# An attention and two-layer kernel whose hand-kept order is computed anew with other prices for DMA and GpSimd

## The chip, the core and the metric

The kernel runs on one core of a Trainium2 chip. The metric is the device time in microseconds of one execution. All work is in 32-bit floats.

## The reference

Attention within chunks of 64 tokens feeds two layers of a feed-forward network without a router. Cut to what is computed:

```python
scores = (1 / sqrt(64)) * q_c @ k_c.T            # 4 x 8 heads, 9 chunks of 64 tokens
attn = softmax(scores); x = attn @ v_c           # 2304 tokens x 512
r = maximum(x @ w_in, 0); x = (s * (r * r) + b) @ w_out        # first layer, 512 -> 2048 -> 512
h = x @ w_in2; g = maximum(h, 0) + log1p(exp(-abs(h)))         # second layer
out = g @ w_out2
```

The weights arrive in 64-bit floats and are converted on the chip.

## The kernel before

**Stages.** The kernel goes through five stages: attention over 18 tiles of 128 tokens (`attention`, `held`), the first product of layer one (`quad0`), its second product (`second`, phase 0), the first product of layer two (`quad1`) and its second product (phase 1). Each product of two matrices is done in blocks with seven products in place of eight, so sums and differences of blocks are made on VectorE (DVE) and GpSimd (POOL), and each operand is split into a high and a low part (`split`: a cast on ScalarE, L1077, and a subtraction, L1086). Meanwhile weights are loaded and converted (`weights1`, `weights2`).

**A quad.** `quad0 i j` (and `quad1 i j`) takes 256 columns of weights, number i of 8, and 384 tokens, group j of 3. Its steps are numbered here in the order in which the function adds them, in brackets. The seven products on TensorE, each of six matmuls (L1487), are [0], [2], [4], [7], [11], [14], [17]; [1], [5] copy a sum to the next bank on ScalarE (L1509); [3] copies it to the buffer `s2` (ScalarE or VectorE, L887 or L889); [6] and [8] subtract on VectorE (L1064). The results leave the banks through ScalarE as [9], [12], [15], [18] (L1520) into buffers of kind `go` (five places; every other quad from number 6 on uses `g1`, in layer two `g2` and `g3`), and are squared in place as [10], [13], [16], [19] (L1532 or L1534). Four adds or subtractions follow, [23] to [26], three of which claim a further buffer. Seven stores of 192 KB to DRAM, [20], [21], [22] and [27] to [30] (L905), free the buffers: that of [9] is free after [24] and store [20]; of [12] after [25] and [21]; of [15] after [26] and [22]; of [18] after store [28]. The second product loads these results again (`second`, step [0], 768 KB).

**What sets the order.** Each function adds steps (`Op`) to a list, 3587 in all, of which 726 are TensorE's. The table `PLAN`, written out in the source, gives each step a rank by its turn and number, with V or G behind it where the step goes to VectorE or GpSimd instead of its default engine. `order` sorts each engine's steps by rank: this is the engine's order, and every engine keeps to it strictly. `order` also steps through a picture of the machine (prices of engines, a DMA queue) to choose which of a kind's places each step gets, and in which interleaving the engines' steps are emitted. All loads and stores are issued by SyncE (SP) on one queue. The loads of `s` and `b` (L1986, L1987, 0.5 KB each, one value to each of 128 partitions) are not ranked: they are emitted behind the last step of `x_ready[0, 2]`, which is `held 8`[11].

Of the kernel before, what the change touches and what calls it, by code (L numbers as in the profile page):

```python
# [610 lines left out]
class Work:  # L611
# [8 lines left out]
    BANKS = "A", "S", "at"  # L620
    HELD = {"DVE": 0.06, "POOL": 0.1}
    STORE, LOAD, FIRST = 1.6, 2.3, 3.0
    BYTES = 330e3

    COLD = 7.0

# [34 lines left out]
    def order(self, places):  # L661
# [7 lines left out]
        memory = port = 0.0  # L669
# [84 lines left out]
def block_attention_two_layers(  # L754
# [36 lines left out]
    work = Work()  # L791
# [462 lines left out]
    held = {}  # L1254
# [799 lines left out]
```

## Time and profile before

| | us |
|---|---|
| median of 3 runs | 813.82 |
| lowest and highest | 811.82, 817.78 |
| the profiled execution | 814.79 |
| its span, first to last instruction | 813.0 |
| TensorE busy | 775.7 (95%) |
| VectorE busy | 671.7 (83%) |
| ScalarE busy | 533.3 (66%) |
| GpSimd busy | 126.1 (16%) |

The profile is of one execution. PE is TensorE, DVE VectorE, ACT ScalarE, POOL GpSimd, SP SyncE, whose queue issues the DMAs. An engine is busy while an instruction of it is executed; the idle time before an instruction is put down to what ended it. An L and a number is a line of the kernel; L1064 and L905 are helpers that many steps share, so a step is told from its neighbours by its place in time and in the order of its engine.

### The profile page before, as it was taken

To read this page: it belongs to the slowest core of one execution; us is meant where nothing else is said; L and a number is where in the kernel's file an instruction comes from. 1 tells how busy PE (TensorE), PEld (TensorE's weight loads), DVE (VectorE), ACT (ScalarE), POOL (GpSimd) and SP (SyncE) were. 2 spreads that over 40 slices of the span, in tenths; PEclk is the share of its full clock that TensorE was granted. 3 is DMA by queue.
4 is the path that set the end of the run, shared out by engine and by line. 5 is a ranking of instruction groups with operands and counts; after the bars stand their busy time and mean duration, and the time that the engine had idled before them with its cause. 6 is when DMAs were issued, how large, how long until landed. Compare 5 with 4: busy or idle time off the path is not lost.

```text
span 813.0 us, 14302 instructions
## 1 busy us (share of the span) xinstructions
PE 775.7 (95%) x4995; PEld 750.5 (92%) x4995; DVE 671.7 (83%) x1181; ACT 533.3 (66%) x1068; POOL 126.1 (16%) x132
## 2 busy tenths in 40 slices
PE   6898899999988799999999899999999999999998
PEld 5687798899987799999999899999999999999997
DVE  6999898999896798987999979999865766567674
ACT  6998888889876777665677856565555455445451
POOL 4444001222212110000104221212200000000000
PEclk9999999999999999999999999999999999999999
DMA  7766388999999997988875068998788897558743
GB/s 243 246 211 211 133 289 252 312 311 326 312 317 298 324 331 307 338 291 286 295 237 193 11 229 297 311 322 266 271 286 291 303 383 257 204 230 267 282 162 136
DMA packets 97112, 214.86 MB, mean 264 GB/s; under 512 B 10384, under 2 KB 70800, under 8 KB 96144
## 3 DMA queue, kind: packets, MB, share of 16 engines
q1 hardware_dynamic: 97040, 213.95, 77.2%
q8 instruction: 39, 0.64, 0.3%
q14 instruction: 33, 0.27, 0.1%
HBM read 128.45 MB, written 85.46 MB: 263 GB/s over the span
## 4 chain that ended last, share of the span: by engine, by line
PE 63%; DVE 8%; DMA 6%; ACT 5%; issue 2%; POOL 0%; SPq 0%; DVEq 0%; ACTq 0%; POOLq 0%
PE S L1755 15%; PE at L1755 15%; PE at L1487 13%; PE A L1755 10%; PE S L1487 6%; DMA summed<-mem 5%; PE A L1487 4%; DVE mem L1064 2%; DVE operands L1086 2%; ACT mem L1520 1%; ACT operands L1077 1%; DMA last<-summed 1%; DVE last L1086 1%; ACT mem L956 1%; ACT mem L1532 1%
## 5 line engine op out<-in xcount | busy, mean ns | idle before, releaser
L1755 PE MATMUL S<-operands 128*128 128x384 f32 (+1 forms) x768 | 176.4, 337 | 4.8 <-ACT mem L1520 4.7
L1755 PE MATMUL at<-operands 128*128 128x384 f32 (+1 forms) x768 | 175.3, 335 | 0.0
L1086 DVE TENSOR_TENSOR operands<-mem,operands 128x768 fp32r<-128x768 f32 (+3 forms) x150 | 132.8, 908 | 41.3 <-ACT operands L1077 40.8
L1077 ACT CAST operands<-mem 128x768 fp32r<-128x768 f32 (+3 forms) x150 | 115.3, 792 | 72.4 <-PE at L1755 39.0
L1064 POOL TENSOR_TENSOR mem<-mem 128x256 f32<-128x256 f32 (+1 forms) x95 | 92.2, 978 | 432.3 <-DVE mem L1044 229.9
L1077 ACT CAST operands<-last 128x768 fp32r<-128x768 f32 (+2 forms) x136 | 103.8, 781 | 81.1 <-PE at L1755 39.2
L1064 DVE TENSOR_TENSOR mem<-mem 128x384 f32<-128x384 f32 (+1 forms) x261 | 131.6, 521 | 25.1 <-DMA summed<-mem 9.5
L1755 PEld LDWEIGHTS S<-operands 128*128 128x128 f32 x768 | 137.3, 189 | 6.4 <-ACT mem L1520 5.3
L1086 DVE TENSOR_TENSOR operands<-last,operands 128x768 fp32r<-128x768 f32 (+2 forms) x132 | 118.5, 914 | 25.0 <-ACT operands L1077 24.2
L1755 PEld LDWEIGHTS at<-operands 128*128 128x128 f32 x768 | 137.7, 189 | 0.0
L1487 PE MATMUL at<-operands 128*128 128x384 f32 x624 | 120.7, 337 | 4.5 <-ACT S L1509 3.5
L1487 PEld LDWEIGHTS at<-operands 128*128 128x128 f32 x624 | 108.5, 188 | 8.3 <-ACT S L1509 4.9
L1755 PE MATMUL A<-operands 128*128 128x384 f32 (+1 forms) x480 | 89.3, 335 | 0.0
L1487 PE MATMUL S<-operands 128*128 128x384 f32 x420 | 85.0, 338 | 2.3 <-DVE S L1064 2.3
L1755 PEld LDWEIGHTS A<-operands 128*128 128x128 f32 x480 | 83.9, 188 | 0.1
L1487 PEld LDWEIGHTS S<-operands 128*128 128x128 f32 x420 | 74.3, 189 | 3.0 <-DVE S L1064 2.7
L1520 ACT ACTIVATE mem<-S 128x384 f32<-128x384 f32 x104 | 50.7, 490 | 36.7 <-DMA summed<-mem 13.8
L1487 PE MATMUL at<-last,operands 128*128 128x384 f32 x336 | 68.6, 341 | 2.9 <-DVE mem L889 1.3
L1487 PE MATMUL A<-operands 128*128 128x384 f32 x300 | 62.5, 346 | 7.2 <-DVE A L1064 4.5
L1487 PEld LDWEIGHTS at<-last,operands 128*128 128x128 f32 x336 | 59.1, 188 | 5.3 <-ACT S L1509 1.8
L1487 PEld LDWEIGHTS A<-operands 128*128 128x128 f32 x300 | 52.7, 191 | 11.3 <-DVE A L1064 5.7
L956 ACT ACTIVATE mem<-mem 128x512 f32<-128x512 int32 x88 | 55.5, 631 | 1.6 <-DVE mem L947 0.8
(101 smaller groups left out, 891.2 us busy)
## 6 DMA issues: line engine op xcount, KB each, us to landing
summed<-mem SPq DMA_DIRECT2D x336, 192.0 KB, 3.6
last<-summed SPq DMA_DIRECT2D x54, 768.0 KB, 5.9
mem<-in_w_dram SPq DMA_DIRECT2D x64, 512.0 KB, 4.9
mem<-summed SPq DMA_DIRECT2D x30, 768.0 KB, 6.2
last<-in_qk_dram SPq DMA_DIRECT2D x36, 256.0 KB, 4.0
forms<-mem SPq DMA_DIRECT2D x16, 512.0 KB, 5.0
mem<-forms SPq DMA_DIRECT2D x7, 1024.0 KB, 7.5
mem<-forms SPq DMA_DIRECT2D x12, 512.0 KB, 6.5
```

What stands on the lines that cost most here:

```text
L956: return lambda e: nc.scalar.activation(out=out(), in_=in_(), func=AF.Prelu, scale=scale, bias=bias, alpha=alpha)
L1064: lambda e: on(e).tensor_tensor(out=out(), in0=x(), in1=y(), op=op or ALU.subtract),
L1077: lambda e: nc.scalar.copy(out=hi().bitcast(F32R), in_=x()),
L1086: lambda e: on(e).tensor_tensor(out=lo().bitcast(F32R), in0=x(), in1=hi(), op=ALU.subtract),
L1487: nc.tensor.matmul(acc(dst)().rearrange("p (u c) -> p u c", u=GROUP), l[a], r[c], start=start and kk == 0 and x == 0, stop=kk == 1 and x == 2,
L1520: lambda e: nc.scalar.activation(out=at(go), in_=acc(place)(), func=AF.Softplus if ph else AF.Relu),
L1532: nc.scalar.activation(out=at(go), in_=at(go), func=AF.Square)
L1755: nc.tensor.matmul(at(accs[d])[:, :width], l[a], r[c], start=i == 0 and y == 0, stop=i == NF - 1 and y == 2,)
```

## The change

The picture of the machine has other prices. A store is taken to land 1.9 us after its data have moved (before 1.6), a load 1.9 (2.3), a load of attention 2.8 (3.0); the queue moves 365 KB/us (330), and a load behind a store costs 0.6 us more. A step on GpSimd is priced higher. `PLAN` is replaced for the most part: ranks and engine marks; the last part of the table stays. Operations and shapes are the same. Of the table, the rows that the prediction speaks of stand here.

```diff
-    STORE, LOAD, FIRST = 1.6, 2.3, 3.0
-    BYTES = 330e3
+    STORE, LOAD, FIRST = 1.9, 1.9, 2.8
+    BYTES, TURN = 365e3, 0.6
...
+        op.store = False
...
                 memory = max(memory, t + cost) + op.late / self.BYTES
+                if stored and not op.store:
+                    memory += self.TURN
+                stored = op.store
...
-    return Port(0.135 + n * (0.0017 if spread else 0.00214))
+    return Port(0.2 + n * (0.0018 if spread else 0.0025))
...
-            op.lag = work.STORE
+            op.lag, op.store = work.STORE, True
...
-    "held 8": "410 433 401 420 394 426 443 438G 432 446 447 457",
+    "held 8": "403 430 405 409 407 415 443 435G 429 439 453 458",
-    "quad0 1 0": "388 397 400 408 411 419 423 430 439 436 445 417 428 434 424 442 450 449 461 464 458 437 454 467 473 475 481 471 477 479 484",
+    "quad0 1 0": "388 396 401 408 412 419 424 428 437 434 438 406 421 445 422 436 441 440 457 460 448 451 444 463 468 473 478 485 471 477 482",
-    "quad0 0 1": "406 440 444 452 456 466 470 474 482 491 496V 468 483 487 480 493 501V 486 495 504 500 503 507 509 515 521 523 513 519 524 528",
+    "quad0 0 1": "433 442 447 456 459 467 470 474 483 490 495V 465 481 484 479 498 504 489 496 501 499 503 508 505 510 519 522 511 516 529 526",
-    "weights2 0 0": "465 494V 497 508 499 505 511 490 516 520 532 525 531 537 543 546 517G 549 553 564 560",
+    "weights2 0 0": "464 491V 492 506 493 497 513 488 518 521 533 523 530 536 542G 549 540 554 561 564 558",
-    "quad0 3 2": "800 809 824 834V 838 844 850 857 866 874 876 843 885 902 883 927 934 877 893 900 881 920 940 910 915 924 941 914 989 928 981",
+    "quad0 3 2": "785 800 816 824 836 858 855 866 874 884 889V 844 892 897 870 900 915 893 909 913V 894 911 947 917 922 931 935 921 930 934 950",
-    "weights1 0 7": "1189 1229 1244 1248 1234 1237 1254 1223 1258 1262 1273 1263 1269 1277 1286 1291 1259G 1290 1282 1287 1292 1296",
+    "weights1 0 7": "1198 1236 1242 1249 1241 1248 1254 1227 1258 1261 1264 1262 1268 1275 1279 1287 1271 1282 1280 1284 1289 1293",
-    "quad0 7 2": "1301 1305 1311 1319 1322 1336 1331 1339 1348 1353 1355V 1315 1327 1332 1345 1357 1377 1356 1364 1367 1360 1335 1400 1371G 1375 1380G 1386 1392 1379 1402 1390",
+    "quad0 7 2": "1299 1305 1308 1313V 1318 1328 1340 1343 1350 1361 1367 1312 1319 1333 1332 1348 1352 1365 1372 1374 1370 1336 1355 1377G 1387 1389 1393G 1397 1395 1392 1400",
-    "quad0 6 0": "1176 1186 1190 1201 1221 1235 1232 1239 1260 1279 1283 1251 1267 1276 1265 1297 1308 1280 1295 1299V 1318 1284 1312 1303 1309 1323 1328G 1307 1314 1326 1443",
+    "quad0 6 0": "1174 1184 1188 1199V 1206 1222 1216 1245 1257 1292 1301 1231 1267 1296 1288 1302 1307 1260 1272 1277 1320 1311 1327 1306 1310G 1316 1329 1309 1317 1324 1366",
-    "quad0 7 0": "1329 1349 1352 1359 1369 1376 1378 1382 1393 1425 1434 1389 1395 1420 1403 1421 1431 1398 1427 1429 1436 1441 1446 1433 1435 1453G 1456 1452 1439 1479 1460",
+    "quad0 7 0": "1338 1344 1349 1369 1371 1376 1379 1386 1394 1431 1436 1381 1399 1404V 1396 1423 1427 1403 1426 1432V 1441 1407 1446 1440 1445G 1462 1464 1443 1449 1465 1470",
-    "quad0 6 1": "1206 1226 1245 1253 1257 1270 1274 1293 1302 1338 1361V 1272 1354 1370 1288 1334 1343 1304 1346 1365V 1368 1458 1394 1384G 1388 1391 1408 1387 1447 1463 1493",
+    "quad0 6 1": "1213 1229 1237 1247 1252 1270 1259 1281 1291 1335 1359V 1265 1339 1342V 1274 1357 1378 1294 1346 1368V 1458 1347 1385 1401 1437 1442 1448 1502 1468 1479 1454",
-    "second0 0 1 2 0": "1366 1414 1419 1424",
+    "second0 0 1 2 0": "1373 1420 1434 1438",
```

## Rows read from the trace of the kernel before

**Rows 1.** The page: the span, and each engine's busy time.
```profile
span 813.0 us, 14302 instructions
...
PE 775.7 (95%) x4995; PEld 750.5 (92%) x4995; DVE 671.7 (83%) x1181; ACT 533.3 (66%) x1068; POOL 126.1 (16%) x132
```

**Rows 2.** Stretches: start:end, length, each engine's busy us, clock, DMA share, GB/s.
```profile
20.00:80.00 60.00, 54.65 (x894) 45.61 (x893) 57.39 (x122) 54.92 (x172) 29.38 (x31) 1.00 0.70 224
80.00:100.00 20.00, 16.03 (x87) 15.17 (x87) 17.44 (x39) 16.59 (x36) 1.83 (x2) 0.98 0.37 128
100.00:240.00 140.00, 135.85 (x750) 131.00 (x748) 128.47 (x244) 118.93 (x248) 26.76 (x26) 0.99 0.93 303
240.00:280.00 40.00, 30.83 (x155) 28.25 (x155) 29.92 (x55) 27.74 (x56) 8.02 (x8) 0.96 0.92 296
280.00:420.00 140.00, 140.00 (x806) 139.86 (x806) 122.47 (x189) 90.12 (x133) 9.70 (x9) 1.00 0.88 312
```

**Rows 3.** The same columns, for the two stretches of lower clock.
```profile
99.10:102.40 3.30, 3.30 (x12) 3.30 (x11) 2.79 (x6) 2.52 (x7) 0.00 (x0) 0.50 0.85 262
...
276.60:279.90 3.30, 3.30 (x12) 3.30 (x11) 2.47 (x4) 3.07 (x6) 0.00 (x0) 0.50 0.94 323
```

**Rows 4.** Timeline of the DMA queue: start, length, line, what is issued.
```profile
90.39 0.48 SPq L1986 DMA_DIRECT2D s_sb<-in_s_dram  x1
90.92 0.60 SPq L1987 DMA_DIRECT2D b_sb<-in_b_dram  x1
91.57 0.59 SPq L905 DMA_DIRECT2D summed<-mem  x1
92.26 0.38 SPq L905 DMA_DIRECT2D mem<-in_w_dram  x1
```

**Rows 5.** Issue to landing: the store of 91.57, that of 90.0, all stores.
```profile
DMA to landing us min/median/max: 4.7/4.7/4.7
...
DMA to landing us min/median/max: 1.9/1.9/1.9
...
summed<-mem SPq DMA_DIRECT2D x336, 192.0 KB, 3.6
```

**Rows 6.** One microsecond of the stretches' table; the last two numbers are the DMA's.
```profile
92.00:93.00 1.00, 1.00 (x8) 1.00 (x7) 1.00 (x3) 1.00 (x3) 0.00 (x0) 1.00 0.05 0
```

**Rows 7.** Timeline about 97 us: VectorE, TensorE, ScalarE; idle before, and its end.
```profile
96.36 0.56 DVE L1064 TENSOR_TENSOR mem<-mem 128x384 f32<-128x384 f32 x1 [2.42 <-DMA summed<-mem]
...
98.25 1.61 PE L1487 MATMUL S<-operands 128*128 128x384 f32 x6 [2.33 <-DVE S L1064]
...
99.54 1.00 ACT L1520 ACTIVATE mem<-S 128x384 f32<-128x384 f32 x2
```

**Rows 8.** Timeline, 260 to 276 us; last the landing of the 260.66 store.
```profile
261.00 0.49 ACT L1520 ACTIVATE mem<-S 128x384 f32<-128x384 f32 x1 [4.70 <-DMA summed<-mem]
...
260.51 0.56 DVE L1064 TENSOR_TENSOR mem<-mem 128x384 f32<-128x384 f32 x1 [1.76 <-DMA summed<-mem]
...
275.43 0.91 PE L1755 MATMUL S<-operands 128*128 128x384 f32 x3 [2.81 <-ACT mem L1520]
...
DMA to landing us min/median/max: 7.5/7.5/7.5
```

**Rows 9.** Timeline of TensorE about 162 and 241 us.
```profile
162.12 1.32 PE L1487 MATMUL at<-last,operands 128*128 128x384 f32 x6 [1.30 <-DVE mem L889]
...
241.54 1.33 PE L1487 MATMUL A<-operands 128*128 128x384 f32 x6 [1.46 <-DVE A L1064]
```

**Rows 10.** Groups by line and shape: count, busy us, mean ns, idle before, releasers.
```profile
L1064 POOL TENSOR_TENSOR mem<-mem 128x256 f32<-128x256 f32 x66 | 58.9, 900 | 348.2 <-DVE mem L1044 229.9 <-DVE mem L1064 79.2 <-DMA last<-summed 23.6
...
L1064 DVE TENSOR_TENSOR mem<-mem 128x384 f32<-128x384 f32 x163 | 93.4, 579 | 23.5 <-DMA summed<-mem 9.5 <-ACT mem L1520 6.1 <-POOL mem L1064 5.5
...
L1064 DVE TENSOR_TENSOR mem<-mem 128x256 f32<-128x256 f32 x98 | 40.4, 425 | 1.6 <-POOL mem L1064 0.6
```

**Rows 11.** The view of waits: who waited for whom, us, times, longest.
```profile
ACT mem L1520 <- DMA summed<-mem: 17.6, 14, 4.7
```

More of the change, by code (lines that the diff above doesn't have):

```diff
@@ L669, in order @@
         memory = port = 0.0
+        stored = False
         taken = float("inf")
```

746 rows, old and new, of the table PLAN are left out of this document.

## Prediction

> **What bounds the kernel now.** I read the page's first parts first: the span, and each engine's busy time [rows 1]. TensorE is busy for 775.7 of 813.0 us, so 37.3 us of idle TensorE, plus whatever the clock takes, is all that an order of the same operations can win or spoil. Next I read the table by stretches, to see where the 37.3 us lie [rows 2]. In the attention stage (20 to 80 us) TensorE is idle for 5.4 us, but VectorE is busy for 57.4 of 60 us and ScalarE for 54.9: there those two bound. From 80 to 100 us TensorE idles for 4.0 us, over the long first layer (100 to 240 us) for 4.2 of 140, and at the change from the first layer to the second product (240 to 280 us) for 9.2 of 40. From 280 to 420 us it has no idle at all: nothing can be won there. Third, the granted clock in two short stretches [rows 3]: 0.50, the 1.2 GHz level, at 99.1 to 102.4 and at 276.6 to 279.9 us, each time just after TensorE had stood still for over 2.3 us. A stretch of 3.3 us at half the clock costs 1.65 us.
>
> Last, the timeline around the longest stalls, for what each was waiting for. The clearest is at 94 us. VectorE stands for 2.42 us until a store lands, and TensorE follows with 2.33 us [rows 7]. The step is `quad0 1 0`[25], which needs a buffer of kind `go` that comes free when store [20] has landed. The queue shows why that is late: [20] is issued at 91.57 us, directly behind the loads of `s` and `b` [rows 4], and takes 4.7 us, while the store issued at 90.0 us, ahead of them, took 1.9 us and the median store 3.6 us [rows 5]. From 92 to 93 us the DMA engines are busy for a share of 0.05 and move 0 GB/s [rows 6], so it is not bandwidth but these two 0.5 KB loads that hold the queue.
>
> **The change, part by part.** The constants and `TURN` issue no instruction. They act through `order`, on the buffer that each step gets and on the interleaving in which `emit` runs. The ranks fix each engine's order.
>
> The engines. Counting the V and G marks and default engines over the 3587 steps, GpSimd falls from 121 to 103 steps (55 go to VectorE, 37 come back), VectorE rises from 1157 to 1167 and ScalarE from 932 to 940. A GpSimd add of 128x256 takes 900 ns, VectorE's 425 and, at 128x384, 579 [rows 10]. For VectorE the 18 net steps off GpSimd are 14 of 256 and 4 of 384: 14 x 0.425 + 4 x 0.579 = 8.3 us, less eight handed to ScalarE at about 0.5 us, 4.0 us: plus 4.3 us. What hides it is VectorE's idle of 11.5 us in 100 to 240 us [rows 2]; with that cover gone it costs 4.3 us. In the attention stage, where VectorE has 2.6 us idle in 60, three 256-wide adds come to it from GpSimd; one copy comes from ScalarE and one goes there. Bounds 0 and 3 x 0.425 = 1.3 us; I take 0.8, since the stage is nearly full.
>
> Place 1, 94 us. `held 8`[11], after which the loads of `s` and `b` are emitted, has rank 458 now (457 before), but store [20] of `quad0 1 0` moves from 458 to 448 and [21] is at 451. So [20] and [21] go ahead of the small loads, and [25], a VectorE step that can begin at 93.9 us, should find its buffer free: at 1.9 us the store lands at about 92.4. What is late next: the two loads now stand in front of `weights2 0 0`[0] (464) and store [28] (471). The ScalarE step at 99.54 us [rows 7], `quad0 0 1`[15], takes the buffer that [28] frees, so it can't come forward by all of 2.3 us. Bounds 0 and 2.33 + 1.65 = 4.0 us; I take 2.5, because two claims in a row find their stores ahead and only the third still waits.
> The Trainium skill (DMA: Bandwidth & Descriptors, section "Queues, rings and completion order") says that each DMA engine consumes descriptors in ring order, so that work queued behind a slow transfer waits for it. The trace agrees (4.7 us behind, 1.9 us ahead). By that rule the delay is handed on, not removed; if [28] then lands no earlier than before, this place gives nothing and the sum is -2.5.
>
> Place 2, 162.1 us. TensorE waits 1.30 us [rows 9] for the copy `quad0 3 2`[3], which stands on VectorE behind a slowed add. It goes to ScalarE, and its product [2] one place earlier on TensorE. Bounds 0 and 1.3; I take 1.0.
>
> Place 3, 241.5 us. TensorE waits 1.46 us [rows 9] for `quad0 6 1`[8], behind a 1.2 us subtraction of `weights1 0 7`[21] and a square. Now [8] has rank 1291 and [21] 1293, and the square `quad0 6 0`[19] is ScalarE's. Bounds 0 and 1.46; I take 1.2.
>
> Place 4, the change of stage. 9.2 us idle less the 1.46 of place 3 is 7.7 us, and 1.65 us of clock, 9.3 in all. ScalarE waits 4.70 us for a store before `quad0 7 0`[12], VectorE 1.76 us before `quad0 6 1`[25], TensorE later 2.81 us [rows 8]. Behind the waiting steps stand subtractions and casts that TensorE needs. Store [22] of `quad0 7 2`, which together with [26] frees the next `go` buffer, is issued only at 260.66 us and takes 7.5 us [rows 8]. In the changed plan [22] has rank 1355, ahead of all loads of the second product (1373 on), and `quad0 6 1`[25] moves from 1391 to 1442, behind the first second product (1438). Both named waits should go. But [20] and [28] of the same quads stay among five loads of 512 and 768 KB, and `quad0 7 0`[15] still needs [28], with splits of the second product behind it on ScalarE. Bounds 0 and 9.3; I take 2.5, about a quarter, since the last and longest stall (2.81 us) is of that kind.
>
> New waits. Counting by rank the claims of the buffers `go`, `g1`, `g2` and `g3`, of those that a store has to set free, 28 come within three TensorE products of its issue before, 27 after (4 and 1 within two). So waits like ScalarE's 17.6 us [rows 11] and VectorE's 9.5 us [rows 10] on stores will be about as many, elsewhere. TensorE's idle in 100 to 240 us that no named place explains, 4.15 - 1.30 = 2.85 us, is dealt anew; bounds 0 and 2.85, I take +1.4, half. From 480 to 813 us I move nothing: the cover is TensorE's own work, as in 280 to 420 us.
>
> Sum: -2.5 - 1.0 - 1.2 - 2.5 + 0.8 + 1.4 = -5.0 us. VectorE's 4.3 us stand at nothing beyond the 0.8, under the idle named. The profiled execution took 814.8 us (span 813.0 and 1.8 around it), so 809.8; the median of the runs, 813.8, is 1.0 lower, so I predict 809.
>
> **The rivals.**
> A, no change: the stalls wander. For it: the claims within three products are as many as before, and the small loads still hold the queue. Against: places 2 and 3 need no DMA. Places 1 and 4 give nothing, 2 and 3 give 2.2 us, the new waits and the attention stage take 2.2: 813.8. It is also the rival that the new picture does nothing for the real queue.
> B, the large gain: places 1 to 3 clear wholly, with the first clock stretch, and place 4 by half. 4.0 + 1.3 + 1.5 + 4.6 = 11.4 us, less 2.2 for the attention stage and the new waits, is 9.2: 804.6. With all of place 4 it is 13.9, so 799.9. For it: the new prices sit nearer the trace: GpSimd at 0.84 us (before 0.68) against 0.90 for 256 [rows 10], a 192 KB store alone at 2.9 us from issue (before 2.65) against 3.6 [rows 5].
> C, slower: VectorE becomes the bound of the first layer. About 16 of the steps taken off GpSimd lie before 300 us; on VectorE they are 16 x 0.5 = 8 us. If its idle there cannot be used, because it is itself waiting for ScalarE and stores, all of it lands on the end and eats the gains: 813.8 + 8 = 822. It decides from the point where less than 8 of the 21.6 us that VectorE idles in 100 to 280 us [rows 2] can be filled. Against: eight squares and copies leave it for ScalarE, which idles 21 us in 100 to 240 us alone.
>
> **How the numbers follow.** Chances: forecast (805 to 812) 0.40, A (812 to 818) 0.23, B (798 to 805) 0.25, C (818 to 826) 0.12. One per cent of 813.8, about what a measurement of this kernel tells from no change, is 8.1 us: faster is below 805.7, slower above 821.9. Faster: B and 0.05 at the forecast's lower edge, 0.30. Slower: a little over half of C, 0.07. Same: the rest, 0.63. The range goes from 800, where all four places are clear (0.07 of B lies below), to 818 (C lies above). The likeliest case alone is 805 to 812.
>
> **What would show it.** Place 1: store [20] lands in about 2 us, no TensorE wait over 1 us between 92 and 100 us, granted clock 1.00 behind it. Places 2 and 3: no wait over 1 us at `quad0 3 2`[4] and `quad0 6 1`[17]. Place 4: ScalarE's 4.70 us gone, TensorE idle in 40 us there below 9.2. Wrong: a new TensorE stall of over 2 us elsewhere, above all with a clock stretch at 0.50 behind it, or VectorE over 96% busy from 100 to 240 us with TensorE waiting for it.

## The result, and the profile after

| | before | after |
|---|---|---|
| median, us (13 runs each) | 814.99 | 807.84 |
| lowest and highest | 810.62, 817.78 | 804.11, 811.91 |
| the profiled execution | 814.79 | 807.13 |

The ratio is 0.991, with a 95% interval of 0.989 to 0.9929: 7.3 us less (5.8 to 9.0). The prediction was 809 us, 5.0 us less, in a range of 800 to 818; so the time and its sign came as forecast, and what has to be asked is whether it came by the steps named.

First the page after, span and busy time (before: [rows 1]).

```profile
span 805.4 us, 14248 instructions
...
PE 776.1 (96%) x4991; PEld 749.4 (93%) x4991; DVE 665.7 (83%) x1191; ACT 536.6 (67%) x1076; POOL 108.1 (13%) x114
```

TensorE does the same work in 7.6 us less, so its idle time has gone from 37.3 to 29.3 us. VectorE's busy time has not risen by the 4.3 us that the prediction counted; it fell by 6.0. That is hardly less work: the durations of its single instructions add up to 742.2 us before and 741.5 after, but the records of neighbouring instructions overlap for 70.5 and 75.8 us, and busy time counts an overlap once. Now the same stretches as in [rows 2]: length, each engine's busy us, clock, DMA share, GB/s.

```profile
20.00:80.00 60.00, 54.80 (x889) 45.28 (x889) 57.49 (x126) 53.98 (x171) 27.22 (x27) 1.00 0.69 218
80.00:100.00 20.00, 18.25 (x98) 17.01 (x99) 19.69 (x43) 19.00 (x41) 1.98 (x2) 1.00 0.49 164
100.00:240.00 140.00, 136.85 (x762) 131.65 (x761) 129.39 (x252) 122.16 (x255) 16.76 (x17) 1.00 0.93 308
240.00:280.00 40.00, 35.39 (x179) 33.20 (x178) 31.58 (x56) 28.78 (x55) 9.02 (x8) 0.91 0.96 322
280.00:420.00 140.00, 139.31 (x797) 137.90 (x797) 120.58 (x191) 91.36 (x135) 6.60 (x7) 1.00 0.87 303
```

From 80 to 100 us TensorE idles for 1.8 us (before 4.0) and the clock is 1.00; from 240 to 280 us for 4.6 us (9.2), but at a mean clock of 0.91 (0.96). Here are the four places. The view of the DMA queue and the timelines of VectorE and TensorE about 94 us, TensorE about 157 us, then ScalarE and TensorE about 256 us; the bracket at the end is the idle time before and what ended it.

```profile
88.58 1.28 SPq L910 DMA_DIRECT2D summed<-mem  x3
89.91 0.48 SPq L1991 DMA_DIRECT2D s_sb<-in_s_dram  x1
90.45 0.61 SPq L1992 DMA_DIRECT2D b_sb<-in_b_dram  x1
...
93.94 0.55 DVE L1069 TENSOR_TENSOR mem<-mem 128x384 f32<-128x384 f32 x1
...
94.08 1.33 PE L1492 MATMUL A<-operands 128*128 128x384 f32 x6 [0.58 <-DVE mem L1069]
...
157.12 1.22 PE L1492 MATMUL at<-last,operands 128*128 128x384 f32 x6
...
254.39 0.49 ACT L1525 ACTIVATE mem<-S 128x384 f32<-128x384 f32 x1 [1.60 <-POOL mem L1069]
...
258.10 2.26 PE L1492 MATMUL at<-operands 128*128 128x384 f32 x6 [1.96 <-DVE mem L1069]
...
269.78 1.03 PE L1760 MATMUL S<-operands 128*128 128x384 f32 x3 [1.46 <-ACT mem L1525]
```

At place 1 the three stores stand ahead of the small loads, and the VectorE step that waited 2.42 us [rows 7] begins at 93.94 with no wait. At place 2 the product `quad0 3 2`[4] begins at 157.12 with none (1.30 before, [rows 9]). At place 4 ScalarE's 4.70 us for a store [rows 8] have become 1.60 us for a GpSimd add; TensorE stands 1.96 and 1.46 us there. Behind the 1.96 us comes the one stretch of half clock in the middle of the run, twice as long as one of before [rows 3]; this is its second half.

```profile
261.50:264.90 3.40, 3.40 (x12) 3.40 (x12) 3.37 (x7) 1.77 (x3) 0.59 (x1) 0.50 0.84 342
```

The view of waits has a large change (before: ScalarE 17.6 us [rows 11], VectorE 9.5 us [rows 10]). Waiting engine and line, releaser, us in total, times, longest:

```profile
ACT mem L1525 <- DMA summed<-mem: 6.6, 10, 1.4
...
DVE mem L1069 <- DMA summed<-mem: 3.8, 6, 1.2
```

Where it changed has to be read by stretches. Here is the same view from 100 to 240 us, before and after, and then behind 430 us, before and after.

```profile
DVE mem L1064 <- DMA summed<-mem: 1.6, 1, 1.6
ACT mem L1520 <- DMA summed<-mem: 1.4, 3, 0.7
...
DVE mem L1069 <- DMA summed<-mem: 2.3, 4, 0.7
ACT mem L1525 <- DMA summed<-mem: 1.8, 3, 0.9
...
ACT mem L1520 <- DMA summed<-mem: 8.8, 7, 4.0
DVE mem L1064 <- DMA summed<-mem: 3.7, 3, 2.3
...
ACT mem L1525 <- DMA summed<-mem: 3.3, 4, 1.4
DVE mem L1069 <- DMA summed<-mem: 0.3, 1, 0.3
```

Of the 27.1 us before, 3.0 are in the long first layer, and they become 4.1. The fall to 10.4 is around places 1 and 4 (11.6 to 2.6 us) and behind 430 us, where the second layer follows (12.5 to 3.6).

To place the gain, count TensorE's 726 steps in their order and compare when the n-th begins. The profiled execution of before lost time in its first 14 us that is no part of the order: a third stretch of half clock, at 10.4 to 13.7 us, which five of the six experiments below that begin in the order of before don't have.

```profile
10.40:13.70 3.30, 3.30 (x20) 2.63 (x16) 2.84 (x9) 3.27 (x19) 0.99 (x2) 0.50 0.68 257
```

So all are set equal at step 24 (42.3 us in before). Times in us against before; e5, e6, e7 and e12 are explained below.

```
step  begins in before   after    e5     e6     e7    e12
  72        92.6         +0.5   +0.4   +0.4    0.0    0.0
  84       109.7         -2.4   -2.6   -2.5   -0.8   -2.6
 120       150.1         -2.7   -0.4   -3.5   -1.0   -2.5
 132       164.3         -4.3   -0.5   -4.8   -1.1   -2.9
 192       230.1         -5.0   -0.2   -6.1   -1.9   -1.9
 204       244.8         -4.9   -0.5   -3.8   -1.8   -2.4
 228       281.4         -7.3   -1.6   -6.6   -3.3   -4.7
 360       419.2         -5.6   -1.6   -6.2   -0.9   -4.7
 480       550.1         -7.3   +0.4   -5.2   -3.0   -5.3
 725       807.9         -7.3   +0.8   -5.4   -3.6   -5.7
```

In the changed kernel: attention +0.5, place 1 -2.9, on to step 120 -0.2, place 2 -1.6, on to step 192 -0.7, place 3 (step 201 in before) +0.1, place 4 -2.4. Behind 281 us nothing is won on balance: 1.7 us are lost by 419 us and won back by 550 us. The sum is the 7.3 us of the measurement.

### The profile page after: what moved, and what is told of

Read it like the earlier page. It is cut to its first block, busy times and chain, and to the rows that moved or that the text cites. A ratio compares the mean times of both kernels' runs of the same rounds, so it can differ in the third digit from the quotient of the medians.

```text
span 805.4 us, 14248 instructions
## 1 busy us (share of the span) xinstructions
PE 776.1 (96%) x4991; PEld 749.4 (93%) x4991; DVE 665.7 (83%) x1191; ACT 536.6 (67%) x1076; POOL 108.1 (13%) x114
## 4 chain that ended last, share of the span: by engine, by line
PE 54%; DVE 6%; DMA 3%; ACT 2%; issue 1%; SPq 0%; POOL 0%; DVEq 0%; ACTq 0%; POOLq 0%
PE S L1760 13%; PE at L1760 13%; PE at L1492 10%; PE A L1760 9%; PE S L1492 6%; PE A L1492 3%; DVE operands L1091 3%; DMA summed<-mem 2%; DVE mem L1069 1%; DVE last L1069 1%; DMA forms<-mem 1%; DMA last<-summed 1%; ACT operands L1082 1%; ACT mem L1525 0%; DVE mem L1049 0%
## 5 line engine op out<-in xcount | busy, mean ns | idle before, releaser
L1069 DVE TENSOR_TENSOR mem<-mem 128x384 f32<-128x384 f32 (+1 forms) x278 | 136.4, 512 | 11.6 <-DMA summed<-mem 3.8
L1069 POOL TENSOR_TENSOR mem<-mem 128x256 f32<-128x256 f32 (+1 forms) x78 | 76.0, 979 | 469.0 <-DVE mem L1049 239.6
L1091 DVE TENSOR_TENSOR operands<-last,operands 128x768 fp32r<-128x768 f32 (+1 forms) x132 | 119.2, 920 | 23.3 <-ACT operands L1082 22.6
```

The source lines that it names most:

```text
L1069: lambda e: on(e).tensor_tensor(out=out(), in0=x(), in1=y(), op=op or ALU.subtract),
L1091: lambda e: on(e).tensor_tensor(out=lo().bitcast(F32R), in0=x(), in1=hi(), op=ALU.subtract),
```

## The experiments

Times against the kernel before are the ratios on record with their 95% interval, turned into us; they are not the ratios of the medians, which give e1 1.9 us less, e2 5.8 us less and e3 0.1 us more. A single profile can be out by 1.7 us for each clock stretch that it happens to have, and by more in the second half of the run: e3, e4 and e10, whose steps there stand in the order of before, end 2.4 us less, 3.5 more and 2.6 less than they stood at step 228. So verdicts go by the times, and places by the profiles. Where ranks are fractions, the steps were numbered anew in that order.

**e1_small_early: place 1 alone.**

```diff
-            if op is x_ready[0, NG - 1][-1]:
+            if getattr(op, "own", "") == "quad0 0 0/28":
                 nc.sync.dma_start(out=s_sb, ...)
```

> The kernel before with one thing moved: the two loads of s and b are emitted behind store quad0 0 0[28] (about 80 us), where the queue then has nothing for some 5 us, and no longer ahead of stores [21] and [20] of quad0 1 0. Order theory (place 1 comes from these two loads standing ahead of two stores): store [20] lands about 2 us after its issue, VectorE's 2.42 us and TensorE's 2.33 us at 94 to 98 us go, the granted clock stays 1.00 behind them; 1.5 to 4 us less than before, most likely 2.5. Rival, relief of GpSimd (18 fewer steps on it) and rival, the constants: neither is in this kernel, so no change, within 0.5 us. If the delay is only handed on along the queue: no change, and a wait of the same length one or two steps later.

Measured: 0.9964 (0.9942 to 0.9987), 2.9 us less. In its profile store [20] lands 2.2 us after its issue, TensorE has no idle time over 0.1 us between 92 and 100 us, and the gain stands at 2.6 us at step 132. The two loads still occupy the queue, now where nobody waits: from 81 to 82 us it moves nothing.

```profile
81.00:82.00 1.00, 1.00 (x8) 1.00 (x7) 1.00 (x4) 1.00 (x3) 0.00 (x0) 1.00 0.05 0
...
238.97 1.48 PE L1487 MATMUL A<-operands 128*128 128x384 f32 x4 [1.44 <-DVE A L1064]
...
239.30:242.50 3.20, 3.20 (x12) 3.20 (x11) 3.17 (x7) 0.69 (x1) 0.97 (x1) 0.50 0.64 207
```

Place 1 is shown: in the order of before the position of two 0.5 KB loads costs about 2.5 us. This profile lost the gain again at 239 us, where place 3's wait stands as in before (1.44 us), this time with half clock behind it; over twelve runs the gain is there.

**e2_small_back: place 1 undone in the changed kernel.**

```diff
-            if op is x_ready[0, NG - 1][-1]:
+            if getattr(op, "own", "") == "quad0 1 0/22":
```

> The changed kernel with one thing undone: the loads of s and b are emitted ahead of stores [20] and [21] of quad0 1 0 again, as in the kernel before. Order theory: the waits at 94 to 98 us come back with the slow clock behind them; 1.5 to 4 us more than the changed kernel, most likely 2.5, so 4 to 5 us less than before. Rivals (GpSimd, constants): as the changed kernel, 7 us less than before.

Measured: 0.9911 (0.9879 to 0.9943), 7.2 us less than before (4.6 to 9.9), the same as the changed kernel. By the time alone the order theory's 4 to 5 us is at the edge of the interval; by the profile it was wrong. The loads hold the queue again with [20] and [21] behind them (in before [20] alone stood behind them, [21] was issued at 87.47 us, ahead), and [20] takes 3.3 us instead of 2.0. But the step that needs it begins without a wait:

```profile
90.00:91.00 1.00, 1.00 (x8) 1.00 (x7) 1.00 (x3) 0.97 (x3) 0.00 (x0) 1.00 0.05 0
...
93.32 0.55 DVE L1069 TENSOR_TENSOR mem<-mem 128x384 f32<-128x384 f32 x1
```

The small loads are issued at 88.32 us, 2.1 us earlier than in before (90.39, [rows 4]), because store [22] ahead of them is. [20] lands at 92.8 and [21] at 93.3, just in time. So the new order mends place 1 twice: the stores stand ahead of the loads, and they are ready earlier. Either alone is enough, the first by e1 in the old order, the second by e2 in the new.

**e3_copy: place 2 alone.**

```diff
-    "quad0 3 2": "800 809 824 834V ...
+    "quad0 3 2": "800 809 824 834 ...
```

> The kernel before with one mark taken off: the copy quad0 3 2[3] is ScalarE's. Order theory for place 2: TensorE's wait of 1.30 us at 162 us goes, and the end comes 0.5 to 1.6 us earlier, most likely 1.0. If place 2 came from GpSimd's relief around 160 us or from the steps being dealt anew: no change, within 0.5 us.

Measured: 0.9988 (0.9964 to 1.0011), 1.0 us less with an interval that holds nothing too. TensorE's wait shrinks from 1.30 to 0.88 us and is now for the same copy on ScalarE:

```profile
159.74 1.33 PE L1487 MATMUL at<-last,operands 128*128 128x384 f32 x6 [0.88 <-ACT mem L887]
```

The mark alone gives a third of the wait. In the changed kernel the wait is gone; the step's rank has also moved from 834 to 824, but no run tries that alone. And the wait is not the order's alone: e10 below has these steps as in before, with the copy on VectorE, and TensorE has 0.1 us of idle time here. The difference is the pair of adds that stands ahead of the copy on VectorE, first in before, then in e10:

```profile
159.09 1.71 DVE L1064 TENSOR_TENSOR mem<-mem 128x256 f32<-128x256 f32 x2
...
158.02 0.89 DVE L1064 TENSOR_TENSOR mem<-mem 128x256 f32<-128x256 f32 x2
```

In before a GpSimd add runs beside them (159.34 to 160.39 us); in e10 it begins at 159.26 us, behind them.

**e4_constants: the new picture without the new ranks.** The plan of before in the code of after.

> The ranks and engines of the kernel before, with the changed constants alone (prices, and the 0.6 us for a load behind a store): they only choose which buffer of a kind a step takes and how the engines' instructions are interleaved. Order theory and GpSimd theory: no change, within 1 us. Constants theory: most of the 7 us.

Measured: 1.0007 (0.9981 to 1.0032). No effect of the constants without the ranks can be told; it lies between 1.5 us less and 2.6 more.

**e5_head, e6_first_part, e7_second_part: splices of the two orders.** Steps below the rank stand in the one order, the rest behind them in the other, each with its engine.

```diff
e5:  order = [x for x in after if x.rank < 600]  + [the rest in the order of before]
e6:  order = [x for x in after if x.rank < 1230] + [the rest in the order of before]
e7:  order = [x for x in before if x.rank < 1200] + [the rest in the order of after]
```

> The changed order up to its rank 600 (TensorE at 117 us), the order of before behind it. Order theory: what the changed kernel has won by then at place 1, 2.5 to 3 us, stays to the end: 2 to 3.5 us less than before. Theory that the gain is handed back at the next stall: within 1 us of before.

> The changed order up to its rank 1230 (TensorE at 223 us), the order of before behind it: places 1 and 2 with the whole first layer, but the old change of stage. Order theory: 5 us less than before at 223 us, and 4 to 5.5 us less at the end. GpSimd theory: about 5 as well (most steps taken off it lie before). Theory that the waits at the change of stage absorb what comes earlier: 0 to 3 us less.

> The reverse: the order of before up to its rank 1200 (TensorE at 222 us), the changed order behind it, so places 3 and 4 alone. Order theory: 2 to 3 us less than before, all of it won between 230 and 275 us. If parts 1 and 2 were the whole gain: no change, within 1 us.

Measured: e5 1.001 (0.9993 to 1.0028), 0.8 us more; e6 0.9957 (0.9939 to 0.9975), 3.5 us less; e7 0.9971 (0.9952 to 0.999), 2.4 us less. The halves add up to 5.9 of the 7.3 us, and the rest is inside the intervals. e6 came out below what was expected, e5 far below. e7 is near its number, but not all at its place: of the 3.6 us in its profile 1.4 are won between steps 192 and 228, and 0.8 at step 84, where it still has a stall (2.65 us) but the clock at 1.00 behind it.

The table shows where: e5 has place 1's 2.6 us at step 84, has lost 2.2 of them by step 120, just behind the splice, and loses 2.4 more between steps 228 and 725, where its steps stand as in before; that is no more than single profiles of one order differ by there (above). Its profile, the slowest of its twelve runs, also has this wait in attention for a load of v, of which the changed kernel has two of 0.5 us and the kernel before none:

```profile
40.51 1.75 PE L1426 MATMUL at<-last 64*64 64x64 f32 x31 [2.70 <-DMA last<-in_v_dram]
```

So a gain at one place is not kept by itself. The new order of attention seems to have a thinner margin on its loads: of six profiles with it three have such waits (after, e5, e6), of eight with the old one none. e6 has won 4.8 us at step 132, meets place 3's wait of before again, and ends at 5.4 in its profile:

```profile
236.58 1.34 PE L1492 MATMUL A<-operands 128*128 128x384 f32 x6 [1.45 <-DVE A L1069]
...
ACT mem L1525 <- DMA summed<-mem: 14.3, 13, 3.0
```

The wait of 1.4 to 1.5 us at place 3 stands in before, e1, e3, e6 and e10, with 1.3 us in e4 and 1.0 in e5, all with the old order there; it is in none with the new one. That the GpSimd theory expected 5 us of e6 as well doesn't tell the two apart; e9 does.

**e8_seed_earlier and e11_fill: the stall that the change left.** In the changed kernel `quad0 7 1`[6] stands behind conversions of weights that are needed much later. e8 moves it and [5]; e11 moves [8] too, and a product that has all its operands ahead of one for which TensorE waits.

```diff
e8, e11 (quad0 7 1)
-    [5] 1414   [6] 1419
+    [5] 1401.5 [6] 1400.5
e11 also
-    quad0 7 1 [8] 1425     second3 0 1 2 3 [0] 1480
+    quad0 7 1 [8] 1412.5   second3 0 1 2 3 [0] 1472.5
```

> The changed kernel with two ranks altered: quad0 7 1[5] (ScalarE) goes ahead of weights1 1 0[9], and quad0 7 1[6] (VectorE) ahead of quad0 7 0[13]. In the changed kernel TensorE stands for 1.96 us at 256 us until [6] is done, and has a granted clock of 0.50 for 6.8 us behind it. Theory that [6] is late only for what stands ahead of it on VectorE and ScalarE, and that the clock falls for the stall: the wait goes and with it the slow stretch, 2 to 5 us less than the changed kernel (most likely 3.5), so about 804.5. If the load that follows (weights 0 1[1], landed at 262 us) sets this stretch anyway: the wait moves on and the end stays within 1 us of the changed kernel.

> The kernel of e8_seed_earlier with two more steps moved: quad0 7 1[8] goes ahead of weights 0 1[3] on VectorE, and on TensorE the product second3 0 1 2 3, which has all its operands, goes ahead of second0 0 1 0 0[3], for which TensorE waits 1.5 us in the changed kernel and 3.35 us in e8. Order theory: the wait at quad0 7 1[17] (2.68 us in e8) goes, and a product of 1.2 us stands inside the next stall; 2 to 4 us less than the changed kernel, about 805. Theory that VectorE's work sets this stretch: the first wait turns into a longer second one, only the product that fills it is won, 0 to 1.2 us less than the changed kernel, about 807.

Measured against before: e8 0.9933 (0.9911 to 0.9955), 5.5 us less; e11 0.9905 (0.9877 to 0.9934), 7.7 us less, 806.0 us. Neither can be told from the changed kernel (7.3). The stall moved on: in e8 it is 2.68 us at the next subtraction and 3.35 us at the second product.

```profile
257.14 1.31 PE L1492 MATMUL A<-operands 128*128 128x384 f32 x6 [2.68 <-DVE A L1069]
...
266.01 1.39 PE L1760 MATMUL S<-operands 128*128 128x384 f32 x3 [3.35 <-ACT mem L1525]
```

The table of stretches tells why. Here is 250 to 270 us in before, after, e8 and e11, in this order; the third busy time is VectorE's.

```profile
250.00:270.00 20.00, 15.63 (x83) 14.26 (x83) 13.45 (x25) 13.43 (x29) 3.00 (x3) 1.00 0.95 320
...
250.00:270.00 20.00, 15.92 (x73) 14.74 (x71) 17.38 (x34) 14.34 (x26) 4.38 (x4) 0.83 0.92 302
...
250.00:270.00 20.00, 13.97 (x68) 13.04 (x67) 19.82 (x37) 15.08 (x28) 3.20 (x3) 0.91 0.97 326
...
250.00:270.00 20.00, 15.39 (x84) 14.21 (x83) 19.25 (x37) 15.46 (x29) 3.21 (x4) 1.00 0.95 319
```

VectorE is busy for 13.5 of 20 us before, 17.4 after, 19.8 in e8: once the waits for stores are gone and [6] comes early, it is full. Moving its steps about then mostly chooses which product waits. My expectation for e8 named a load as the next bound; it was VectorE. e11 gains 2.2 us by step 228 and has no half clock there, and hands back 2.5 us by step 252, in part in waits for splits on VectorE and ScalarE. e8 keeps no lead either: it is 2.4 us ahead of the changed kernel at step 204, before the moved steps, 1.9 ahead at step 228, and 1.0 behind at step 360.

**e9_engines: the engines without the ranks.** The V and G marks of after on the ranks of before, with the constants of before.

> The ranks and constants of the kernel before, with the changed kernel's choice of engine for every step (160 marks differ; 18 steps net off GpSimd, ScalarE takes the copy of place 2). Relief theory (GpSimd's slow adds were what held the steps up): most of the 7 us, 4 us or more less than before. Order theory: place 2 alone, 0 to 1.5 us less, and the marks without the ranks that go with them bring new waits, so 1 us less to 3 us more. Rival C of the prediction (VectorE as the bound): 4 us or more above before.

Measured: 1.0151 (1.0117 to 1.0185), 12.3 us more. GpSimd is relieved as in after (109.6 us busy), and the waits for stores rise; TensorE's longest is the last of these.

```profile
PE 780.7 (95%) x5002; PEld 751.2 (91%) x5002; DVE 673.6 (82%) x1191; ACT 538.0 (65%) x1076; POOL 109.6 (13%) x114
...
ACT mem L1520 <- DMA summed<-mem: 22.2, 14, 4.3
...
278.77 0.69 PE L1755 MATMUL S<-operands 128*128 128x384 f32 x1 [4.75 <-ACT mem L1520]
```

The relief theory is out as a cause by itself: the marks alone win nothing, and e12 below wins most of the gain without taking a step off GpSimd. That relief adds to the gain together with the ranks is not excluded; place 2's wait hangs on a GpSimd add (e3). The time falls on the side of the prediction's rival C, but not by its mechanism: from 100 to 240 us VectorE is busy for 126.97 us, less than before.

**e10_place4: place 4 alone.**

```diff
 quad0 7 2
-    [16] 1377     [22] 1400
+    [16] 1357.5   [22] 1360.5
 quad0 6 1
-    [25] 1391     [26] 1408
+    [25] 1424.3   [26] 1424.6
```

> The kernel before with place 4's two causes alone undone: quad0 7 2[16] and its store [22] come forward (ranks 1377 and 1400 to 1357.5 and 1360.5, ahead of the second product's loads), and quad0 6 1[25] and [26] go behind second0 0 1 2 0[2]. Order theory: ScalarE's 4.70 us before quad0 7 0[12] and VectorE's 1.76 us before quad0 6 1[25] go, TensorE's stalls of 1.69, 1.84 and 2.81 us shrink by 2 to 3 us in all; 1.5 to 4 us less than before, most likely 2.5. Theory that VectorE, busy without a pause from 250 to 270 us in the changed kernel, sets this stretch: the named waits go, TensorE's stalls come back somewhere behind them, and the end stays within 1 us of before.

Measured: 0.9973 (0.9951 to 0.9995), 2.2 us less. Store [22] lands at 255.9 us in 2.6 us (7.5 before, [rows 8]), and both waits for stores are gone. It was not [22] that ended ScalarE's 4.70 us in before, but store [28] (issued at 255.84 us, landed in 5.1): `quad0 7 0`[12] has there the buffer that [28] frees, and with [22] early, here and in the changed kernel, the one that [22] frees. ScalarE still stands 4.07 us before `quad0 7 0`[12], but for a product; of TensorE's three stalls the first is gone and the others are 1.89 and 3.41 us.

```profile
260.42 0.49 ACT L1520 ACTIVATE mem<-S 128x384 f32<-128x384 f32 x1 [4.07 <-PE S L1487]
...
265.40 0.99 PE L1755 MATMUL S<-operands 128*128 128x386 f32 x3 [1.89 <-ACT mem L1520]
...
274.50 0.90 PE L1755 MATMUL S<-operands 128*128 128x384 f32 x3 [3.41 <-ACT mem L1520]
```

This is the order theory's number, though ScalarE's wait did not go, it changed its reason. By steps the profile agrees between 204 and 228, where 2.5 us are won; 1.9 had been lost between 192 and 204, with a half-clock stretch behind place 3's wait that before doesn't have.

**e12_four_places: all four, and nothing else.** e1, e3 and e10 together, and for place 3:

```diff
-    quad0 6 1 [8] 1302    quad0 6 0 [19] 1299V
+    quad0 6 1 [8] 1295.5  quad0 6 0 [19] 1299
```

> The kernel before with the four named places mended by hand and nothing else: the two small loads as in e1, the copy as in e3, quad0 6 1[8] ahead of weights1 0 7[21] with the square quad0 6 0[19] on ScalarE (place 3), and [22], [25], [26] as in e10. Eight steps out of 3587 and two loads. Theory that the changed kernel's gain is made at these four places and adds up: 5.5 to 8 us less than before, as the changed kernel (7). Theory that it is made by the whole order, and that a wait taken away alone is mostly handed back by the next: 1 to 4.5 us less, no more than the best single place (e1, 2.9).

Measured: 0.9937 (0.9912 to 0.9962), 5.1 us less (3.1 to 7.2), between what the two theories expected; the interval reaches into both. Seven steps out of 3587 (the expectation's eight was a miscount) and two loads make about 70% of the change's 7.3 us, near the sum of the places taken singly (2.9 + 1.0 + 2.2 = 6.1, without place 3). The rest is missing earlier: by the table 1.2 us between steps 120 and 132, where e12 still waits 0.9 us for the copy as e3 does, and 1.7 from there to step 192. ScalarE's waits for stores fall only from 17.6 to 13.6 us, where the changed kernel has 6.6, but 9.4 of e12's are behind 430 us, where the changed kernel wins nothing on balance.

```profile
ACT mem L1520 <- DMA summed<-mem: 13.6, 17, 3.0
```

## Why the prediction was right, and where it was not

**Place 1** (predicted -2.5): -2.9 in the profile, -2.9 by e1. The step held. Of what the profile of before loses there, 1.65 us is the half clock of [rows 3], which e3 doesn't have behind the same stall (last section). Whether the delay would be handed on along the queue was left open: nothing paid for it. The load `weights2 0 0`[0] behind the small loads lands in 3.8 us, as in e1, where they are not ahead of it (before 5.3), and store [28] at 96.3 us, 2 us before it is needed. The Trainium skill (DMA: Bandwidth & Descriptors, section "Queues, rings and completion order") says that each DMA engine takes its descriptors in ring order. That work behind a slow transfer waits for it is the prediction's own conclusion, and e2 bears it out: two stores behind the small loads wait while nothing moves.

**Place 2** (-1.0): -1.6 between the two profiles. The order's share of it is not shown: the mark alone carries 0.4 us of the 1.30 by e3's profile and nothing clear of noise in its time, and e10 has the wait not at all with the old steps. The prediction read the cause rightly (a slowed add), but not that it comes and goes.

**Place 3** (-1.2): +0.1. Its 1.46 us wait is gone, but two products later TensorE stands 0.80 us at 236 us for a copy on ScalarE, and between steps 192 and 204 nothing is won. The term was mis-sized: the wait was handed on.

**Place 4** (-2.5): -2.4 by the steps, 2.2 us by e10. The change reaches it by less idle time (7.7 to 4.6 us between steps 204 and 228) and more half clock. In the prediction's account of the cause the freed buffer was right and the store that ended the wait was not (e10).

**Attention** (+0.8): +0.5.

**New waits** (+1.4): the step that failed. It counted by rank how many claims come within three products of the store that frees their buffer (28 before, 27 after), concluded that waits for stores would be as many, elsewhere, and let them cost half of TensorE's unexplained idle time. In the first layer, where the term belongs, the waits were as many (3.0 us before, 4.1 after on VectorE and ScalarE). The price was wrong: the stretches between the named places gave 0.9 us instead of costing 1.4, with 1.5 us of TensorE's idle time there (before 2.5). What made this gain stays open. For the whole run the conclusion failed too: the waits fell from 27.1 us to 10.4. The count knows how soon a claim follows its store's issue, not how long that store takes: [20] took 4.7 us behind two small loads, [22] 7.5 us among the second product's loads. Those are places 1 and 4; the fall behind 430 us goes with no gain on balance, and why the stores came in time there is not shown.

The forecast of 5.0 us less and the 7.3 measured differ by just this term; the errors of the others cancel, which is luck, place 3's above all. So do two errors in what the prediction moved nothing for: 1.7 us lost between 281 and 419 us, where before has no idle time, and 1.7 won back by 550 us. One of its signs of being wrong did come, a new stall of over 2 us elsewhere, for a copy on ScalarE (before: 0.94 and 1.37 us at 454 and 460 us); the clock stays at 1.00 behind it, while e2 has half clock behind the same stall.

```profile
447.29 1.50 PE L1492 MATMUL at<-operands 128*128 128x384 f32 x7 [2.03 <-ACT S L1514]
```

**The counting of engines** held: e9, with the new marks on the old ranks, has 3.9 us more of VectorE instructions than before (746.1 us added up singly), and 4.3 were counted. The changed kernel has 0.7 us less than before; which of its ranks make up the difference was not tried.

**The rivals.** A (the stalls wander) is out by e1, e10 and e12, though e5 shows that it can happen to a part. B (804.6) asked for 1.5 us of place 3 and 4.6 of place 4; the two gave 2.3. C (VectorE becomes the bound) did not happen in the first layer (129.39 us busy of 140, TensorE 136.85), but VectorE is nearly full in 250 to 270 us, and e8 and e11, which fill it, end no earlier than the changed kernel by their times. What stays open: which of the many small changes of rank make the last 2 us that e12 lacks (they lie between steps 120 and 192), and why e5 loses its gain just behind the splice.

## What to carry to other kernels

Look at what stands ahead of a store in its queue, not only at how long before the claim it is issued; two loads of 0.5 KB cost 2.5 us by their position in one order and nothing in another, where the stores were ready earlier. A wait that is taken away is worth what the next one leaves of it: mend a place, then read the engine's busy share in that stretch, and stop moving steps where an engine is full. Choice of engine and order are one decision; half of such a change can cost more (12 us) than the whole gains (7 us).

## What the hardware showed that was not expected

The clock does not follow from the length of a stall. The same stall of TensorE at 95 to 97 us left the clock at 1.00 in e3 and was followed by half clock in e10. Each such stretch of about 3.4 us costs 1.7 us, so two profiles of one order can differ by that alone.

```profile
96.67 1.32 PE L1487 MATMUL S<-operands 128*128 128x384 f32 x6 [2.38 <-DVE S L1064]
...
96.70:100.10 3.40, 3.40 (x18) 3.06 (x18) 3.26 (x7) 3.21 (x9) 0.00 (x0) 1.00 0.69 226
...
97.40 1.41 PE L1487 MATMUL S<-operands 128*128 128x384 f32 x5 [2.41 <-DVE S L1064]
...
98.20:101.40 3.20, 3.20 (x12) 3.20 (x11) 2.83 (x6) 2.40 (x6) 0.00 (x0) 0.50 0.87 293
```

An add on VectorE can take more than twice its time beside one on GpSimd: in the changed kernel 1.25 us at 264.67, against a mean of 565 ns for this shape, while GpSimd adds from 264.31 to 265.50. Most are not so slow: of the adds in this group 20 overlap GpSimd's work, with a mean of 663 ns, and three of them take over 1 us; the other 147 take 552 ns on average and 560 at most.

```profile
264.67 1.25 DVE L1069 TENSOR_TENSOR mem<-mem 128x384 f32<-128x384 f32 x1
...
264.31 1.19 POOL L1069 TENSOR_TENSOR mem<-mem 128x384 f32<-128x384 f32 x1 [6.15 <-DVE mem L1069]
...
L1069 DVE TENSOR_TENSOR mem<-mem 128x384 f32<-128x384 f32 x167 | 93.0, 565 | 10.7 <-DMA summed<-mem 3.8 <-ACT mem L1525 3.5 <-POOL mem L1069 2.1
```

The Trainium skill (SBUF — State Buffer, section "Who interferes with whom") has such a rule: a VectorE instruction with two inputs in SBUF contends with a GpSimd instruction that reads SBUF; this row and the pair of adds at place 2 agree with it. VectorE's lower busy time is for the most part another matter, the closer sequence of its instructions (in the section on the result); e9 has the same marks, and VectorE is busy there for 673.6 us, more than before (671.7).
